# Attention's opening in pieces: halves of K and of the rotation table, Q in two parts, pair 1's Q on GpSimd

## The chip, the cores and the metric

The kernel runs on one core of a Trainium2 chip. The metric is the time of one execution in device microseconds; lower is better. Three executions of the kernel before took 981.68, 982.01 and 981.80 us, median 981.8.

## The reference

The reference is attention with rotary positions, then a mixture of experts that sends each token to one expert, then a dense two-layer block. All is in float32. Cut to what matters here:

```
q_rot, k_rot = rotate(q), rotate(k)          # x1*cos - x2*sin, x1*sin + x2*cos
scores = scale * q_rot @ k_rot.T             # batch 4, 8 heads, 576 tokens, 64 wide
attn = exp(scores - max(scores)); attn /= sum(attn) + 1e-9
x = moe(attn @ v)                            # argmax expert of 8, relu, weighted by its gate
out = relu(x @ w_in)**2 @ w_out              # 2304 tokens, 512 -> 2048 -> 512
```

## The kernel before

The heads are worked off in 16 pairs (P = 0 to 15), two heads on 128 partitions. Q and K of a pair arrive as one block `qk` of 128 x 2 x 2 x 640: the first 2 is the plain copy and the copy with halves swapped, the second is K (index 0) and Q (index 1). `rotate` multiplies both copies with the table `TB` (two `times`) and adds them (one `plus`), in place. The table's Q side is made on ACT from its K side, scaled and moved by 64 columns.

For precision each rotated block is split into a rounded part (`high`, on ACT, into `XH`) and the rest (`low`, into `XL`, on GpSimd unless another engine is named). For pairs 1 and up, `stack_up` lays the parts of one head over each other by ten DMAs on SP's queue (`kZ`, `qZ`, `QH`), so that one matmul does two products. Pair 0 does without: `direct_high` and `direct_low` write its Q parts in place, and its scores take three matmuls instead of two.

Scores come in nine groups s (0 to 3 head 0, 4 to 7 head 1, 8 the last 64 rows of both heads). Each group goes into one of two PSUM buffers `ps` of two banks; VectorE (DVE) takes the row maximum (`smax`, L286), ACT the exponential with its sum (`sexp`, L293), which frees the buffer. Then TensorE (PE) transposes the exponentials (`turn`, L301 and L311), DVE or ACT copies them out (`turned`, L327 and L329), and the product with V follows.

The order on every engine is written out by a list: `at(t, f)` puts a step at a planned time, the list is worked off by time, and each engine runs its instructions strictly in that order. `OFF` has the planned offsets within a pair and the pair's length, 15.954. What `prepare` issues comes ahead of the list. Queues that matter: ACT's order has `high` of pair 2 (planned at 32.143) between pair 1's first maximum (32.353, on DVE) and its first exponential (33.433); GpSimd's (POOL's) order has pair 1's low part and then the three rotation operations of pair 2 (planned from 20.629); SP's has the loads and the stack copies. From pair 2 on, POOL rotates both K and Q of a pair at once, 1280 columns an operation.

In the opening (`prepare`) the table is loaded on ACT's queue and pair 0's K and Q in two transfers on SP's, then pair 1 in one. DVE rotates K, then Q of pair 0, makes the low parts, and rotates pair 1 whole (L433 and L429 are the lines of `times` and `plus`, L425 that of `minus`) ahead of the first row maximum. PE meanwhile runs 14 dummy matmuls (`warm`), and each group of scores of pair 0 has two more ahead of its own (L266).

Of the kernel before, what the change touches and what calls it, by code (L numbers as in the profile page):

```python
# [10 lines left out]
F32 = mybir.dt.float32  # L11
# [48 lines left out]
def shape_constants():  # L60
# [27 lines left out]
    for b in range(B):  # L88
        for c in range(4):
# [21 lines left out]
           un=[32.589, 32.153, 35.217, 38.036, 36.617, 23.748, 28.906, 37.6, 35.653, 34.253, 33.817],  # L111
           out=[33.418, 34.148, 36.917, 39.025, 37.411, 29.788, 32.958, 38.405, 36.294, 35.538, 34.643],
           av=[41.194, 44.969], x=[46.747, 47.789], pj=54.426, fin=58.03)
ON_DVE = [(0, 0), (0, 3), "LQ", "CR", (1, 0), (1, 1), (1, 3)]


def attention(tc, rope, ident, qk, v, w_gate, xd, on_batch, later, ahead):
# [24 lines left out]
    def ppt(name, shape=(128, 512)):  # L142
        return psa.tile(list(shape), F32, name=name, tag="pp", bufs=4)

    def prepare():
        nc.scalar.dma_start(out=TB[:, :, 0], in_=rope)
        load(0)
        load(1)
        for t in Xs:
            nc.gpsimd.memset(t[:, 576:640], 0.0)  # L150
        for t in SS:
            nc.gpsimd.memset(t[:, :, 1:2], 1e-9)
        for two in QH:
            for j in range(2):
                nc.gpsimd.memset(two[j][64 - 64 * j:128 - 64 * j].bitcast(F32), 0.0)
        nc.gpsimd.memset(R, 0.0)
        for r in range(2):
            d = slice(64 * r, 64 * r + 64)
            nc.gpsimd.tensor_copy(R[d, :, r, 0:64], ident[d, d].unsqueeze(1).broadcast_to([64, 4, 64]))
        for o, lo, hi in ((0, 64, 640), (576, 0, 64)):  # L160
            nc.scalar.activation(TB[:, :, 1, o:o + hi - lo], TB[:, :, 0, lo:hi], AF.Copy, scale=0.125)
        for j in range(2):
            Z = T["qZ", j] = zp.tile([128, 640], F32R, name="qZ", tag="qZ", bufs=4)
            nc.gpsimd.memset(Z[64 - 64 * j:128 - 64 * j, 0:512].bitcast(F32), 0.0)
        rotate(0, 0, nc.vector)
        high(0, 0)
        w = ppt("warm")
        for i in range(14):
            nc.tensor.matmul(w, T["hi", 0][:, 0, 0:128], T["hi", 0][:, 0, 0:512], start=True, stop=True)
        rotate(0, 1, nc.vector)  # L170
        direct_high(0)
        low(0, 0, nc.vector)
        direct_low(0, nc.vector)
        load(2)
        rotate(1, None, nc.vector)
        high(1)
        low(1)
        load_v(0)
        stack_up(1)

    def direct_high(P):


        x, h = T["qk", P], T["hi", P]
        for j in range(2):
            r = slice(64 * j, 64 * j + 64)
            nc.scalar.activation(QH[P][j][r], x[r, 0, 1, 0:512], AF.Copy)
        nc.scalar.activation(h[:, 1, 512:640], x[:, 0, 1, 512:640], AF.Copy)

    def direct_low(P, eng):  # L190
        x = T["qk", P]
        for j in range(2):
            r = slice(64 * j, 64 * j + 64)
            minus(eng, T["qZ", 2 * P + j][r, 0:512], x[r, 0, 1, 0:512], QH[P][j][r].bitcast(F32))
        minus(eng, T["lo", P][:, 1, 512:640], x[:, 0, 1, 512:640], T["hi", P][:, 1, 512:640].bitcast(F32))

    def gate_weights():
        for r in range(2):
# [3 lines left out]
    def load(P):  # L202
        t = T["qk", P] = ldp.tile([128, 2, 2, 640], F32, name="qk", tag="qk", bufs=2)
        src = qk[P].rearrange("p (w n c) -> p w n c", w=2, n=2)
        if P == 0:
            for n in range(2):
                nc.sync.dma_start(out=t[:, :, n], in_=src[:, :, n])
        else:
            nc.sync.dma_start(out=t, in_=src)

# [1 line left out]
        V = T["V", P] = wp.tile([128, 2, 5, 64], F32, name="V", tag="V", bufs=2)  # L212
        nc.sync.dma_start(out=V, in_=v[P].rearrange("p (h c d) -> p h c d", h=2, c=5))

    def rotate(P, n, eng, step=None):
        x, a = T["qk", P], slice(0, 2) if n is None else slice(n, n + 1)
        for i, (f, o, y) in enumerate(((times, 0, TB[:, 0, a]), (times, 1, TB[:, 1, a]), (plus, 0, x[:, 1, a]))):
            if step in (None, i):
                f(eng, x[:, o, a], x[:, o, a], y)

    def high(P, n=None):

        if ("hi", P) not in T:
            T["hi", P] = zp.tile([128, 2, 640], F32R, name="XH", tag="XH", bufs=2)
        a = slice(0, 2) if n is None else slice(n, n + 1)
        nc.scalar.activation(T["hi", P][:, a], T["qk", P][:, 0, a], AF.Copy)

    def low(P, n=None, eng=None):
        if ("lo", P) not in T:
            T["lo", P] = zp.tile([128, 2, 640], F32R, name="XL", tag="XL", bufs=2)  # L230
        a = slice(0, 2) if n is None else slice(n, n + 1)
        args = T["lo", P][:, a], T["qk", P][:, 0, a], T["hi", P][:, a].bitcast(F32)
        if eng is None:
            nc.gpsimd.tensor_sub(*args)
        else:
            minus(eng, *args)

    def stack_up(P, n=None):

        h, l = T["hi", P].bitcast(F32), T["lo", P].bitcast(F32)  # L240
        for j in range(2):
            r = slice(64 * j, 64 * j + 64)
            q = nc.scalar if P == 0 and j == 1 else nc.sync
            if n != 1:
                Z = T["kZ", 2 * P + j] = zp.tile([128, 640], F32R, name="kZ", tag="kZ", bufs=4)
                for i in range(2):
                    q.dma_start(out=Z[64 * i:64 * i + 64].bitcast(F32), in_=h[r, 0])
            if n != 0:
                Z = T["qZ", 2 * P + j] = zp.tile([128, 640], F32R, name="qZ", tag="qZ", bufs=4)
                q.dma_start(out=Z[0:64].bitcast(F32), in_=h[r, 1])  # L250
                q.dma_start(out=QH[P % 2][j][r].bitcast(F32), in_=h[r, 1, 0:512])
                q.dma_start(out=Z[64:128].bitcast(F32), in_=l[r, 1])

    def scores(P, s):

        t = T["S", P, s] = ps.tile([128, 2, 512], F32, name="ps", tag="ps", bufs=2)
        if s < 8:
            j, c = divmod(s, 4)
            todo, qs, qh = [j], slice(c * 128, c * 128 + 128), QH[P % 2][j]
            qh = qh[:, qs]  # L260
        else:
            todo, qs, qh = [0, 1], slice(512, 640), T["hi", P][:, 1, 512:640]
        k0 = 0 if s in (4, 5, 6, 7) else 64
        if P == 0:
            for u in range(2):
                nc.tensor.matmul(t[:, u, 0:288], QH[0][0][:, 0:128], T["hi", 0][:, 0, 0:288], start=True, stop=True)  # L266
            H, L = T["hi", P], T["lo", P]
            ql = L[:, 1, 512:640] if s == 8 else T["qZ", 2 * P + j][:, qs]
            for i, (q1, k1) in enumerate(((qh, H), (ql, H), (qh, L))):
                for u in range(2):  # L270
                    nc.tensor.matmul(t[:, u, 0:288], q1, k1[:, 0, k0 + 288 * u:k0 + 288 * u + 288], start=i == 0, stop=i == 2)
            return
        for i, j in enumerate(todo):
            Q1, K1 = T["qZ", 2 * P + j], T["kZ", 2 * P + j]
            for u in range(2):
                nc.tensor.matmul(t[:, u, 0:288], Q1[:, qs], K1[:, k0 + 288 * u:k0 + 288 * u + 288], start=i == 0, stop=False)  # L276
        for u in range(2):
            nc.tensor.matmul(t[:, u, 0:288], qh, T["lo", P][:, 0, k0 + 288 * u:k0 + 288 * u + 288], start=False, stop=True)  # L278
# [103 lines left out]
            at(t, lambda: route(P, t))  # L382

    prepare()
    at(24.0, gate_weights)
    for P in range(NPAIR):
        def on(o, f, *args):
            at(OFF["pair"] * P + o, lambda: f(*args))

        if P > 2:  # L390
            on(OFF["load"], load, P)
        if P > 0:
            on(OFF["v"] + (1.8 if P == NPAIR - 1 else 0), load_v, P)
        if P > 1:
            for i in range(3):
                on(OFF["rope"] + 2.93 * i, rotate, P, None, nc.gpsimd, i)
            on(OFF["hi"], high, P)
            on(OFF["lo"], low, P)
            on(OFF["z"], stack_up, P)
        for s in range(9):  # L400
            on(OFF["S"][s], scores, P, s)
            on(OFF["max"][s], smax, P, s)
            on(OFF["exp"][s], sexp, P, s)
        for un, o, o2 in zip(UNITS, OFF["un"], OFF["out"]):
            on(o, turn, P, un)
# [18 lines left out]
def minus(v, out, a, b):  # L424
    v.tensor_tensor(out=out, in0=a, in1=b, op=ALU.subtract)  # L425
# [839 lines left out]
```

## Time and profile before

| | |
|---|---|
| profiled execution | 982.04 us |
| its span | 980.2 us |
| mean granted clock | 0.997 |
| PE busy | 953.8 us (97%) |
| DVE busy | 531.9 us (54%) |
| ACT busy | 421.5 us (43%) |
| POOL busy | 322.5 us (33%) |

The span is the time from the first to the last instruction of the profiled execution. PE is busy nearly all the time; of the 40 slices of the page only the first has PE at four tenths. The opening is the first 35 us. The four phases after it (the pair loop, routing, experts, dense block) are not touched by the change.

### The profile page before, as it was taken

Reading aid. Unit: us, or ns where it says so; the run is one execution under the profiler, and the core shown is the slowest. Engines: PE = TensorE matmul, PEld = TensorE weight load, DVE = VectorE, ACT = ScalarE, POOL = GpSimd, SP = SyncE. Lnnn points to the kernel's source line nnn. Section 1 sums busy time; section 2 is a strip of 40 time slices with the busy share of each in tenths; the row PEclk is TensorE's granted clock in tenths of the full one; section 3 lists DMA queues with packets and bytes.
Section 4 is the critical chain, followed back from the end, with each engine's and each line's share of the span. In section 5 each row is a group of like instructions: output and inputs, shape, how many; then the busy total and the mean of one; then the engine's idle time right before and its main releaser. Section 6 shows DMA issues by size and latency. Waiting matters only on the chain. (4 is left out here: it accounts for less than half of the span.)

```text
span 980.2 us, 15407 instructions
## 1 busy us (share of the span) xinstructions
PE 953.8 (97%) x5519; PEld 818.1 (83%) x5519; DVE 531.9 (54%) x937; ACT 421.5 (43%) x835; POOL 322.5 (33%) x259
## 2 busy tenths in 40 slices
PE   4999999999999999999999999999999999999997
PEld 4787878788787888888877789999999999999996
DVE  5677877777867255683776479522323323223222
ACT  3676757575642233343464367522222322222221
POOL 4776887887485111251344300010000100100101
PEclk9999999999999999999999999999999999999999
DMA  6876776866542833365377423100100101100000
GB/s 230 238 201 194 231 212 188 256 178 165 183 130 92 303 114 128 107 215 174 130 271 239 160 90 129 33 33 1 38 28 1 65 1 32 34 1 1 33 1 32
DMA packets 45134, 119.80 MB, mean 122 GB/s; under 512 B 8176, under 2 KB 8176, under 8 KB 42608
## 3 DMA queue, kind: packets, MB, share of 16 engines
q1 hardware_dynamic: 39808, 101.58, 33.6%
q0 software_dynamic: 4960, 16.43, 4.9%
q8 instruction: 45, 0.74, 0.3%
q10 hardware_dynamic: 272, 0.66, 0.2%
q14 instruction: 49, 0.40, 0.1%
HBM read 79.93 MB, written 15.11 MB: 97 GB/s over the span
## 5 line engine op out<-in xcount | busy, mean ns | idle before, releaser
L1088 PE MATMUL o<-Wo,gs 128*128 128x512 f32 x864 | 214.5, 393 | 0.0
L1067 PE MATMUL h<-xs,Wi 128*128 128x384 f32 x1008 | 189.6, 336 | 0.0
L1067 PEld LDWEIGHTS h<-xs,Wi 128*128 128x128 f32 x1008 | 178.1, 188 | 6.6
L1088 PEld LDWEIGHTS o<-Wo,gs 128*128 128x128 f32 x864 | 160.0, 188 | 28.3
L1076 DVE SCALAR_TENSOR_TENSOR g<-h,r 128x384 f32<-128x384 f32 x80 | 44.6, 557 | 190.7 <-ACT r L1072 190.7
L293 ACT ACTIVATE e<-ps,mx 128x576 f32<-128x576 f32 x144 | 106.2, 740 | 83.7 <-DVE mx L286 83.5
L1106 POOL DMA_INDIRECT out_dram<-os,at x18 | 17.8, 986 | 369.5 <-DVE os L1101 309.9
L286 DVE TENSOR_REDUCE mx<-ps 128x1 f32<-128x576 f32 x144 | 105.9, 753 | 57.9 <-PE ps L278 50.4
L1072 ACT ACTIVATE r<-h 128x384 f32<-128x384 f32 x96 | 47.1, 490 | 204.7 <-PE h L1067 204.7
L890 PE MATMUL p_y<-W,hh 128*128 128x512 f32 x504 | 123.2, 399 | 1.4 <-ACTq L902 0.8
L861 PE MATMUL p_h<-W,xs 128*128 128x512 f32 x480 | 114.9, 395 | 0.0
L890 PEld LDWEIGHTS p_y<-W,hh 128*128 128x128 f32 x504 | 93.1, 188 | 23.1 <-ACTq L902 1.1
L861 PEld LDWEIGHTS p_h<-W,xs 128*128 128x128 f32 x480 | 88.5, 188 | 18.5 <-DVEq L902 0.7
L311 PE MATMUL pp<-ident,e 128*128 128x128 f32 x640 | 85.4, 273 | 1.3 <-DVE eT L327 1.0
L1078 DVE TENSOR_TENSOR gs<-g,gs 128x384 fp32r<-128x384 f32 x96 | 53.6, 558 | 56.0 <-ACT gs L1077 55.4
L433 POOL TENSOR_TENSOR qk<-qk,TB 128x1280 f32<-128x1280 f32 x28 | 81.4, 2924 | 0.0
L311 PEld LDWEIGHTS pp<-ident,e 128*128 128x128 f32 x640 | 74.4, 141 | 2.6 <-DVE eT L327 1.6
L1077 ACT ACTIVATE gs<-g 128x384 fp32r<-128x384 f32 x96 | 50.4, 525 | 50.4 <-DVE g L1076 49.9
L276 PE MATMUL ps<-kZ,qZ 128*128 128x288 f32 x300 | 71.5, 328 | 0.3
L338 PE MATMUL av<-eT,V 128*64 128x288 f32 x512 | 69.1, 412 | 0.0
L327 DVE COPY eT<-pp 128x512 f32<-128x512 f32 x96 | 64.3, 684 | 4.6 <-PE pp L311 2.7
L895 POOL DMA_INDIRECT yd<-yo,idx x21 | 21.2, 1012 | 124.8 <-DVE yo L894 90.4
(239 smaller groups left out, 1212.2 us busy)
## 6 DMA issues: line engine op xcount, KB each, us to landing
qk<-in_qk_dram SPq DMA_DIRECT2D x15, 1280.0 KB, 7.0
raw<-in_moe_w_dram SPq DMA_DIRECT2D x30, 512.0 KB, 6.5
kZ<-XH SPq DMA_DIRECT2D x60, 160.0 KB, 2.7
rawa<-in_moe_w_dram SPq DMA_DIRECT2D x18, 512.0 KB, 3.9
w<-in_moe_w_in_dram SPq DMA_DIRECT2D x8, 1024.0 KB, 5.2
w<-in_moe_w_out_dram SPq DMA_DIRECT2D x8, 1024.0 KB, 4.9
V<-in_v_dram SPq DMA_DIRECT2D x16, 320.0 KB, 3.0
qZ<-XH SPq DMA_DIRECT2D x30, 160.0 KB, 2.8
```

The costliest lines, as they stand in the source:

```text
L276: nc.tensor.matmul(t[:, u, 0:288], Q1[:, qs], K1[:, k0 + 288 * u:k0 + 288 * u + 288], start=i == 0, stop=False)
L286: nc.vector.tensor_reduce(small("mx", P, 9)[:, s:s + 1], T["S", P, s][:, :, 0:288], axis=AX.XY, op=ALU.max, negate=True)
L293: nc.scalar.activation(ed.rearrange("p (u n) -> p u n", u=2), T["S", P, s][:, :, 0:288], AF.Exp, bias=T["mx", P][:, s:s + 1], accum_out=SS ...
L311: nc.tensor.transpose(t[:, c * 128:c * 128 + 128], src, ident)
L327: nc.vector.tensor_copy(o, i)
L338: nc.tensor.matmul(t[64 * j:64 * j + 64], V[:, j, kc], eT[:, j, kc, cs] if kc < 4 else eL[:, cs], start=kc == 0, stop=kc == 4)
L433: v.tensor_tensor(out=out, in0=a, in1=b, op=ALU.mult)
L861: nc.tensor.matmul(t[u], s[:, a, k], W1[:, b, k, 512 * u:512 * u + 512], start=n == 0, stop=n == 11)
L890: nc.tensor.matmul(t, s[:, a, k], W2[:, b, k], start=n == 0, stop=n == 23)
L1067: nc.tensor.matmul(t, W[:, a, k, fs], s[:, c, k], start=n == 0, stop=n == 11)
L1078: nc.vector.tensor_sub(gs[:, 1], g, gs[:, 0].bitcast(F32))
L1088: nc.tensor.matmul(self.T["o", b][c], gs[:, a, 128 * c:128 * c + 128], W[:, w], start=(f == 0 and n == 0), stop=(f == 15 and n == 2))
```

## The change

- The table is loaded in two halves of 320 columns on ACT's queue; its Q side is made in three pieces instead of two.
- Pair 0's K is loaded in two halves of 320 columns, its Q as part A (256 columns) and part Z (384). Pair 1 is loaded as two transfers, Q first.
- DVE rotates pair 0's K by halves, ACT makes its high part by halves. After the first half come 16 dummy matmuls of 320 columns instead of 14 of 512.
- Q's part A is rotated and split in `prepare`; part Z in the new list `opening`, which has the scores, maxima and exponentials of pair 0 in another order (0, 1, 4, 5, 8, 2, 3, 6, 7) and all of it early in the list.
- The first maxima stand ahead of pair 1's rotation. Pair 1's Q is rotated on POOL (640 columns an operation), its K on DVE in three steps between maxima. High and low parts of pair 1 are made for Q and K apart, the K ones behind the seventh exponential.
- The two dummy matmuls of each group of scores come behind it instead of ahead.
- Four transposes of pair 0 (`FIRST`) move ahead of pair 1's first scores.
- The stack copies of pair 1 issue Q's before K's.

```diff
+FIRST = [(0, 1), (0, 0), (1, 3), (1, 2)]
...
+    HALF, A, Z = (slice(0, 320), slice(320, 640)), slice(0, 256), slice(256, 640)
...
-        nc.scalar.dma_start(out=TB[:, :, 0], in_=rope)
+        for h in HALF:
+            nc.scalar.dma_start(out=TB[:, :, 0, h], in_=rope[:, :, h])
...
-        for o, lo, hi in ((0, 64, 640), (576, 0, 64)):
+        for o, lo, hi in ((0, 64, 320), (256, 320, 640), (576, 0, 64)):
             nc.scalar.activation(TB[:, :, 1, o:o + hi - lo], TB[:, :, 0, lo:hi], AF.Copy, scale=0.125)
...
-        rotate(0, 0, nc.vector)
-        high(0, 0)
-        w = ppt("warm")
-        for i in range(14):
-            nc.tensor.matmul(w, T["hi", 0][:, 0, 0:128], T["hi", 0][:, 0, 0:512], start=True, stop=True)
-        rotate(0, 1, nc.vector)
-        direct_high(0)
+        for h in HALF:
+            rotate(0, 0, nc.vector, cols=h)
+            high(0, 0, h)
+            if h is HALF[0]:
+                T["warm"] = ppt("warm")
+                for i in range(16):
+                    warm(320)
+        rotate(0, 1, nc.vector, cols=A)
+        direct_high(0, A)
         low(0, 0, nc.vector)
-        direct_low(0, nc.vector)
-        load(2)
-        rotate(1, None, nc.vector)
-        high(1)
-        low(1)
-        load_v(0)
-        stack_up(1)
+        direct_low(0, nc.vector, A)
+
+    def warm(n):
+        nc.tensor.matmul(T["warm"][:, 0:n], T["hi", 0][:, 0, 0:128], T["hi", 0][:, 0, 0:n], start=True, stop=True)
+
+    def opening():
...
+        two = lambda s: (lambda: scores(0, s), lambda: smax(0, s), lambda: sexp(0, s))
+        S, M, X = [dict(zip(range(9), [two(s)[n] for s in range(9)])) for n in range(3)]
+        step = lambda i: lambda: rotate(1, 0, nc.vector, i)
+        return [S[0], S[1], lambda: rotate(0, 1, nc.vector, cols=Z), lambda: direct_high(0, Z), M[0], X[0], M[1], X[1],
+                lambda: direct_low(0, nc.vector, Z), lambda: load(2), lambda: rotate(1, 1, nc.gpsimd),
+                S[4], S[5], M[4], X[4], M[5], X[5], step(0), S[8], S[2], M[8], X[8], step(1), lambda: high(1, 1), lambda: low(1, 1),
+                M[2], X[2], step(2), S[3], S[6], M[3], X[3], lambda: high(1, 0), lambda: low(1, 0), lambda: load_v(0), lambda: stack_up(1),
+                M[6], X[6], S[7], M[7], X[7]]
...
-        if P == 0:
-            for n in range(2):
-                nc.sync.dma_start(out=t[:, :, n], in_=src[:, :, n])
+        if P < 2:
+            for n, c in ([(0, h) for h in HALF] + [(1, A), (1, Z)] if P == 0 else [(1, slice(0, 640)), (0, slice(0, 640))]):
+                nc.sync.dma_start(out=t[:, :, n, c], in_=src[:, :, n, c])
...
         if P == 0:
-            for u in range(2):
-                nc.tensor.matmul(t[:, u, 0:288], QH[0][0][:, 0:128], T["hi", 0][:, 0, 0:288], start=True, stop=True)
             H, L = T["hi", P], T["lo", P]
...
+            for u in range(2):
+                warm(288)
             return
...
     prepare()
+    for n, f in enumerate(opening()):
+        at(.1 * n, f)
...
-        for s in range(9):
+        for s in range(9) if P else ():
...
+            if P == 0 and un in FIRST:
+                o, o2 = [t + .2 * FIRST.index(un) for t in (29.5, 29.6)]
```

## Rows read from the trace of the kernel before

**Rows 1.** Busy time by stretch: stretch, length, busy time (instructions) per engine, granted clock, DMA.
```profile
core 0: us, PE busy (x) PEld busy (x) DVE busy (x) ACT busy (x) POOL busy (x), PEclk, DMA share, GB/s
...
50.00:66.00 16.00, 16.00 (x128) 13.04 (x127) 11.81 (x26) 10.52 (x25) 11.17 (x5) 1.00 0.71 194
```

**Rows 2.** Timeline of PE and its weight loads, pair 1's scores s = 8 and 4.
```profile
33.42 0.80 PE L276 MATMUL ps<-kZ,qZ 128*128 128x288 f32 x4
...
35.30 0.30 PEld L276 LDWEIGHTS ps<-kZ,qZ 128*128 128x128 f32 x2 [0.17 <-ACT e L293]
```

**Rows 3.** Timeline of ACT, high part of pair 2.
```profile
33.27 1.26 ACT L226 ACTIVATE XH<-qk 128x1280 fp32r<-128x1280 f32 x1
```

**Rows 4.** Timeline of POOL: pair 1's low part, pair 2's rotation.
```profile
19.90 2.92 POOL L234 TENSOR_TENSOR XL<-qk,XH 128x1280 fp32r<-128x1280 f32 x1 [13.48 <-ACT XH L226]
22.78 5.83 POOL L433 TENSOR_TENSOR qk<-qk,TB 128x1280 f32<-128x1280 f32 x2
28.68 2.94 POOL L429 TENSOR_TENSOR qk<-qk 128x1280 f32<-128x1280 f32 x1
```

**Rows 5.** Timeline of DVE in the opening.
```profile
6.95 1.56 DVE L433 TENSOR_TENSOR qk<-qk,TB 128x640 f32<-128x640 f32 x2 [5.96 <-DMA qk<-in_qk_dram]
...
12.40 1.40 DVE L425 TENSOR_TENSOR qZ<-qk,QH 64x512 fp32r<-64x512 f32 x2
13.83 0.29 DVE L425 TENSOR_TENSOR XL<-qk,XH 128x128 fp32r<-128x128 f32 x1
14.04 2.89 DVE L433 TENSOR_TENSOR qk<-qk,TB 128x1280 f32<-128x1280 f32 x2
...
18.37 1.41 DVE L286 TENSOR_REDUCE mx<-ps 128x1 f32<-128x576 f32 x2
```

**Rows 6.** DMA from 5 to 5.5 us (pair 0) and 8 to 9 (pair 1).
```profile
DMA packets 79, 0.20 MB, mean 404 GB/s; under 512 B 0, under 2 KB 0, under 8 KB 79
...
DMA packets 44, 0.45 MB, mean 451 GB/s; under 512 B 0, under 2 KB 0, under 8 KB 0
```

**Rows 7.** Timelines of DVE and POOL in the experts, where both subtract.
```profile
415.57 1.22 DVE L839 TENSOR_TENSOR W<-rawa,W 128x1024 fp32r<-128x1024 f32 x1 [0.26 <-ACT W L838]
416.57 2.49 POOL L839 TENSOR_TENSOR W<-rawa,W 128x1024 fp32r<-128x1024 f32 x1 [5.92 <-ACT W L838]
417.52 2.63 DVE L839 TENSOR_TENSOR W<-raw,W 128x1024 fp32r<-128x1024 f32 x1 [0.72 <-ACT W L838]
419.02 1.19 POOL L893 COPY yo<-idx 128x16 int32<-128x16 int32 x1
...
499.32 3.60 DVE L839 TENSOR_TENSOR W<-raw,W 128x1024 fp32r<-128x1024 f32 x1
499.42 2.41 POOL L839 TENSOR_TENSOR W<-raw,W 128x1024 fp32r<-128x1024 f32 x1
```

**Rows 8.** Timelines of DVE, ACT and PE, pair 0's scores at full clock.
```profile
28.70 0.76 DVE L286 TENSOR_REDUCE mx<-ps 128x1 f32<-128x576 f32 x1 [0.80 <-PE ps L271]
...
29.49 0.74 ACT L293 ACTIVATE e<-ps,mx 128x576 f32<-128x576 f32 x1 [0.72 <-DVE mx L286]
...
29.18 0.42 PE L271 MATMUL ps<-XH,QH 128*128 128x288 f32 x2
29.45 0.43 PE L271 MATMUL ps<-XH,qZ 128*128 128x288 f32 x2
...
31.75 0.76 DVE L286 TENSOR_REDUCE mx<-ps 128x1 f32<-128x576 f32 x1 [0.81 <-PE ps L271]
```

**Rows 9.** PE's timeline after its gap, and busy time by us around the lower clock.
```profile
20.53 0.53 PE L266 MATMUL ps<-XH,QH 128*128 128x288 f32 x2 [2.56 <-ACT e L293]
...
21.00:22.00 1.00, 1.00 (x9) 1.00 (x8) 0.11 (x1) 0.20 (x2) 1.00 (x1) 0.87 0.88 202
...
25.00:26.00 1.00, 1.00 (x9) 1.00 (x9) 0.35 (x1) 0.41 (x2) 1.00 (x2) 0.92 0.88 233
```

**Rows 10.** Timeline of SP's queue and DMA issues, stack copies of pair 1.
```profile
23.35 1.24 SPq L247 DMA_DIRECT2D kZ<-XH  x2
...
kZ<-XH SPq DMA_DIRECT2D x4, 160.0 KB, 2.4
```

More of the change, by code (lines that the diff above doesn't have):

```diff
@@ L155, in prepare @@
                 nc.gpsimd.memset(two[j][64 - 64 * j:128 - 64 * j].bitcast(F32), 0.0)
+        for j in range(2):
+            q = T["qZ", j] = zp.tile([128, 640], F32R, name="qZ", tag="qZ", bufs=4)
+            nc.gpsimd.memset(q[64 - 64 * j:128 - 64 * j, 0:512].bitcast(F32), 0.0)
         nc.gpsimd.memset(R, 0.0)
@@ L159, in prepare @@
             nc.gpsimd.tensor_copy(R[d, :, r, 0:64], ident[d, d].unsqueeze(1).broadcast_to([64, 4, 64]))
-        for o, lo, hi in ((0, 64, 640), (576, 0, 64)):
+        for o, lo, hi in ((0, 64, 320), (256, 320, 640), (576, 0, 64)):
             nc.scalar.activation(TB[:, :, 1, o:o + hi - lo], TB[:, :, 0, lo:hi], AF.Copy, scale=0.125)
-        for j in range(2):
-            Z = T["qZ", j] = zp.tile([128, 640], F32R, name="qZ", tag="qZ", bufs=4)
-            nc.gpsimd.memset(Z[64 - 64 * j:128 - 64 * j, 0:512].bitcast(F32), 0.0)
@@ L165, in prepare @@
-        rotate(0, 0, nc.vector)
-        high(0, 0)
-        w = ppt("warm")
-        for i in range(14):
-            nc.tensor.matmul(w, T["hi", 0][:, 0, 0:128], T["hi", 0][:, 0, 0:512], start=True, stop=True)
-        rotate(0, 1, nc.vector)
-        direct_high(0)
-        low(0, 0, nc.vector)
-        direct_low(0, nc.vector)
-        load(2)
-        rotate(1, None, nc.vector)
-        high(1)
-        low(1)
-        load_v(0)
-        stack_up(1)
-    def direct_high(P):
+        for h in HALF:
[5 more added lines that the diff above has]
+                    warm(320)
@@ L184, in direct_high @@
+    def direct_high(P, cols):
         x, h = T["qk", P], T["hi", P]
+        to = min(cols.stop, 512)
         for j in range(2):
             r = slice(64 * j, 64 * j + 64)
-            nc.scalar.activation(QH[P][j][r], x[r, 0, 1, 0:512], AF.Copy)
-        nc.scalar.activation(h[:, 1, 512:640], x[:, 0, 1, 512:640], AF.Copy)
-    def direct_low(P, eng):
+            nc.scalar.activation(QH[P][j][r, cols.start:to], x[r, 0, 1, cols.start:to], AF.Copy)
+        if cols.stop > 512:
+            nc.scalar.activation(h[:, 1, 512:640], x[:, 0, 1, 512:640], AF.Copy)
@@ L191, in direct_low @@
+    def direct_low(P, eng, cols):
         x = T["qk", P]
+        to = min(cols.stop, 512)
         for j in range(2):
             r = slice(64 * j, 64 * j + 64)
-            minus(eng, T["qZ", 2 * P + j][r, 0:512], x[r, 0, 1, 0:512], QH[P][j][r].bitcast(F32))
-        minus(eng, T["lo", P][:, 1, 512:640], x[:, 0, 1, 512:640], T["hi", P][:, 1, 512:640].bitcast(F32))
+            minus(eng, T["qZ", 2 * P + j][r, cols.start:to], x[r, 0, 1, cols.start:to], QH[P][j][r, cols.start:to].bitcast(F32))
+        if cols.stop > 512:
+            minus(eng, T["lo", P][:, 1, 512:640], x[:, 0, 1, 512:640], T["hi", P][:, 1, 512:640].bitcast(F32))
@@ L213, in load_v, with rotate, high @@
         nc.sync.dma_start(out=V, in_=v[P].rearrange("p (h c d) -> p h c d", h=2, c=5))
-    def rotate(P, n, eng, step=None):
+    def rotate(P, n, eng, step=None, cols=slice(0, 640)):
         x, a = T["qk", P], slice(0, 2) if n is None else slice(n, n + 1)
-        for i, (f, o, y) in enumerate(((times, 0, TB[:, 0, a]), (times, 1, TB[:, 1, a]), (plus, 0, x[:, 1, a]))):
+        for i, (f, o, y) in enumerate(((times, 0, TB[:, 0, a, cols]), (times, 1, TB[:, 1, a, cols]), (plus, 0, x[:, 1, a, cols]))):
             if step in (None, i):
-                f(eng, x[:, o, a], x[:, o, a], y)
-    def high(P, n=None):
+                f(eng, x[:, o, a, cols], x[:, o, a, cols], y)
+    def high(P, n=None, cols=slice(0, 640)):
         if ("hi", P) not in T:
@@ L225, in high @@
         a = slice(0, 2) if n is None else slice(n, n + 1)
-        nc.scalar.activation(T["hi", P][:, a], T["qk", P][:, 0, a], AF.Copy)
+        nc.scalar.activation(T["hi", P][:, a, cols], T["qk", P][:, 0, a, cols], AF.Copy)
     def low(P, n=None, eng=None):
@@ L236, in low, with stack_up @@
             minus(eng, *args)
-    def stack_up(P, n=None):
+    def stack_up(P):
         h, l = T["hi", P].bitcast(F32), T["lo", P].bitcast(F32)
@@ L242, in stack_up @@
             r = slice(64 * j, 64 * j + 64)
[L243 to L252, printed above, removed]
+            k = T["kZ", 2 * P + j] = zp.tile([128, 640], F32R, name="kZ", tag="kZ", bufs=4)
+            q = T["qZ", 2 * P + j] = zp.tile([128, 640], F32R, name="qZ", tag="qZ", bufs=4)
+            todo = [(q[0:64], h[r, 1]), (QH[P % 2][j][r], h[r, 1, 0:512]), (q[64:128], l[r, 1])]
+            ks = [(k[64 * i:64 * i + 64], h[r, 0]) for i in range(2)]
+            for o, i in todo + ks if P == 1 else ks + todo:
+                nc.sync.dma_start(out=o.bitcast(F32), in_=i)
     def scores(P, s):
```

## The prediction

> **What bounds the kernel now.** I read the page, then the busy table by stretches, then each engine's timeline up to 36 us. The table shows TensorE (PE) busy 16.00 of 16 us in a stretch of the pair loop [rows 1], so once the loop runs, what arrives late stays late and what arrives early stays early. The change touches only the opening, so the question is when that full stretch begins. PE's timeline shows it: pair 1's scores for s = 8 start at 33.42, and those for s = 4 start at 35.30 after a short wait for ACT [rows 2]. I take the start of pair 1's s = 4 as the gauge, **G = 35.30**. In both versions the same work lies before it on PE: pair 0's nine scores, its LQ, CR and the four transposes of FIRST, and pair 1's s = 2 and s = 8. After it the order is the same. So the change is worth the shift of G, and a transpose done earlier gains nothing if G does not move.
>
> G hangs on ACT: the s = 4 scores need the PSUM buffer that the exp of pair 1's s = 2 reads, and in ACT's order that exp stands right behind high(2), which ran from 33.27 to 34.53 [rows 3]. high(2) needs pair 2's rotated Q and K: three GpSimd (POOL) operations of some 2.9 us each that ended at 31.62, queued behind pair 1's low part, which ran from 19.90 [rows 4]. Thus POOL was 1.65 us ahead of ACT. Whoever comes last at high(2), ACT or POOL, sets G, 0.77 us after the end of high(2).
>
> **The change part by part.**
>
> *Loads by halves.* K's two halves carry the bytes of before; K's reader started at 6.95 then [rows 5]. Runs of 2560 bytes (79 packets, 0.20 MB) moved 404 GB/s, runs of 10240 bytes 451 [rows 6]. A straight line through the time per run gives about 357 for runs of 1280 bytes, which puts K's second half near 7.4; with no loss it is 6.95. I take 7.0, by the row. The Trainium skill (DMA: Bandwidth & Descriptors, Specifications) states that line rate is reached from 512 bytes up. The two rows differ by a tenth far above that size, so the trace doesn't quite agree. By the rule K is there at 6.95, by the line at 7.4, and the sum moves by under half a us.
>
> *DVE up to the first maximum.* 640 columns took 0.78 us (two in 1.56), 512 took 0.715 from start to start, 128 took 0.21 [rows 5]; that makes about 0.42 for 320, 0.36 for 256 and 0.50 for 384. From 7.0: K's second half, three operations of 320, 1.3 (8.3); Q's part A, three of 256, 1.1 (9.4); low of K 0.8 (10.2); the two low parts of A 0.7 (10.9); Q's part Z, three of 384, 1.5 (12.4). In the new order the first maximum stands behind all of these, so DVE alone would reach it at 12.4, against 18.37 before [rows 5]. The warm matmuls start when ACT has K's first half and end near 11.7 by my estimate (16 of 320 columns at the lower clock), so they don't hold it.
>
> *Pair 1's Q on GpSimd.* Three operations, each half of 2.92 us: 4.4 us on an engine that was idle there. But DVE does not run beside it. A DVE subtraction with two SBUF inputs, 1.22 us at 415.57, took 2.63 when it started at 417.52 inside a POOL subtraction that ran until 419.06; then DVE ran, and POOL's next copy (16 columns) took until 420.21. One that started at 499.32 took 3.60 because a POOL subtraction started at 499.42 [rows 7]. So two such operations exclude each other and take turns. Q of pair 1 is the fourth transfer; two of 0.66 MB after K's, at 0.41 MB/us, put it near 10. DVE then still has the low of K, two low parts and three rotation steps, all with two SBUF inputs, and all three POOL operations fall between them: first maximum at 12.4 + 4.4 = 16.8. Bounds 12.4 (nothing lost) and 16.8; a gain is excluded, since DVE loses no work before its first maximum by it. I take 16.8, by the three cases.
>
> *From there to the exp of s = 3.* K's high of pair 1 stands on ACT behind the seventh exp. Two PSUM buffers alternate; before, every second maximum came 3.05 us after the first (28.70 to 31.75), with the two dummy matmuls ahead of each score taking 0.27 [rows 8]. They move behind, so a round is 2.78. The exp starts 0.79 after its maximum and takes 0.74 [rows 8]. The seventh is in the fourth round: 3 x 2.78 + 0.79 + 0.74 = 9.9. DVE's steps on pair 1's K (0.8 each) and ACT's high of its Q (0.74) stick out of a round by some 0.45: 10.3. ACT's high of Q's part Z, 1.1 us behind the rotation, delays the first exp by 0.35. And PE stands idle between the second scores and the first exp, from about 14 to 19: before, after 2.56 idle us that ended at 20.53, the granted clock fell to 0.50 (1.2 GHz) at about 21.74 and rose at about 25.16 [rows 9]. That is 3.4 us at half speed, of which I charge a quarter, 0.8, since PE is not all the bound here. 16.8 + 10.3 + 0.35 + 0.8 = 28.3.
>
> *POOL then.* K's high on ACT 0.85 with its wait, K's low on POOL half of 2.92 and the handing over: 30.7. Only now does pair 2's rotation start, since it stands behind both low parts in POOL's queue: 30.7 + 8.84 = 39.55 (before 22.78 + 8.84 = 31.62 [rows 4]). ACT is at high(2) some 7 us earlier and waits; behind it wait the exp, the PSUM buffer and PE. high(2) ends at 39.55 + 0.05 + 1.26 = 40.85, against 34.53: **6.3 us late**.
>
> *PE's clock again.* The stack copies of pair 1 now have K's high (29.2) in front of seven of the ten: 0.62 us each to issue, 2.4 to land [rows 10], the last near 36. s = 8 runs then, and PE waits to 41.6, longer than the gap that brought half clock before. 3.4 us of it in a stretch that PE bounds cost half: **1.7 us** (bounds 0, if the clock holds, and 2.3).
>
> Sum 6.3 + 1.7 = 8.0. The profiled execution took 982.04 (span 980.2), 0.24 above the median of 981.8, so I forecast 981.8 + 8.0 = **989.8 us**.
>
> What I cost at nothing: the table's extra activation (some 0.3 us) lies in ACT's wait for DMA; if it did not, the warm matmuls would start that much later, and they have 0.3 us to spare. load(2) and V issue on SP ahead of the stack copies, whose data come later; without that cover they cost two issues, 1.2 us.
>
> **Rivals.**
>
> *DVE goes first.* If DVE's queued operations keep POOL out, the first maximum is at 12.4 and POOL's three run beside the maxima, which read PSUM. K's low then ends at 12.4 + 0.35 + 10.3 + 2.4 = 25.5, the rotation at 34.3, high(2) at 35.6: 1.1 late, and PE still waits about 5 us ahead of s = 4, 1.7 more: 984.6 (982.9 without the clock). For it: no row has a long chain on DVE against POOL. Against it: at 499.32 DVE was there first and still waited [rows 7]. The Trainium skill (SBUF — State Buffer, Who interferes with whom) says that issue order decides who blocks; by that DVE, always queued, would go first here and the time would be this rival's. The row at 499.32 speaks against it.
>
> *No change.* POOL is blocked in part and PE keeps its clock, so that high(2) comes within 1.9 us of before: 981 to 983.7.
>
> *Faster.* The stall at high(2) does not arise. Its place is the end of K's low on POOL, its point 24.4 (34.53 - 1.31 - 8.84). Every us below that is gained, until the stack copies hold s = 8: they would land near 31, 33.42 - 31 = 2.4, so at best 979.4. For it the first maximum must come by 11.3 and nothing collide; DVE's chain alone ends at 12.4, so K's second half would have to be there at 5.9, ahead of its bytes at the rate of before, or the maxima closer than the round above.
>
> *Halves don't come sooner.* If both halves land together, warm matmuls and first scores start a us later and DVE's end at 12.4 stays, since it hangs on the second half: inside the range.
>
> **How the numbers follow.** Forecast (they take turns, 987 to 992): 0.62. DVE first or mostly so (983.8 to 987): 0.20. No change (979.9 to 983.7): 0.11. Faster: 0.07. A measurement of this kernel can tell about 0.2% from no change, 1.96 us; so slower 0.82, same 0.11, faster 0.07. The range 983 to 992 leaves out faster, most of no change and a tail above: under 2 in 10.
>
> **What would show it.** In the profile after: DVE operations of 1.8 us and more beside three POOL operations between 10 and 17; the first maximum near 17; pair 2's first rotation on POOL at 30 or later; high(2) on ACT behind an idle stretch that POOL ends; PE idle for several us ahead of pair 1's s = 4, then half clock. The forecast is wrong if K's low on POOL ends before 26 or s = 4 starts before 37. If DVE's operations keep their lengths, the 4.4 us are wrong; if PE's gaps close the delay after 42, so is the claim that the loop keeps what the opening loses.

## The result: 989.5 us, 0.8% slower, by way of GpSimd's queue

| | before | after |
|---|---|---|
| median (lowest to highest of 4) | 981.90 us (981.68 to 982.54) | 989.45 us (988.00 to 990.12) |
| profiled execution, its span | 982.04, 980.2 | 988.00, 986.2 |
| mean granted clock | 0.997 | 0.993 |

The ratio is 1.0076, 95% interval [1.0064, 1.0088]: slower, 0.35 us below the forecast of 989.8.

DVE and POOL after, in the opening (timelines: start, duration, engine, line, operation, idle time and its releaser):

```profile
7.42 0.90 DVE L452 TENSOR_TENSOR qk<-qk,TB 128x320 f32<-128x320 f32 x2 [0.40 <-DMA TB<-in_rope_dram]
...
10.62 2.10 DVE L444 TENSOR_TENSOR qZ<-qk,QH 64x256 fp32r<-64x256 f32 x2
12.76 3.64 DVE L452 TENSOR_TENSOR qk<-qk,TB 128x384 f32<-128x384 f32 x2
16.43 0.56 DVE L448 TENSOR_TENSOR qk<-qk 128x384 f32<-128x384 f32 x1
16.90 1.41 DVE L301 TENSOR_REDUCE mx<-ps 128x1 f32<-128x576 f32 x2
...
25.92 1.98 POOL L253 TENSOR_TENSOR XL<-qk,XH 128x640 fp32r<-128x640 f32 x1 [9.94 <-ACT XH L245]
28.71 1.55 POOL L253 TENSOR_TENSOR XL<-qk,XH 128x640 fp32r<-128x640 f32 x1 [0.82 <-DMA QH<-XH]
30.22 5.76 POOL L452 TENSOR_TENSOR qk<-qk,TB 128x1280 f32<-128x1280 f32 x2
36.06 2.89 POOL L448 TENSOR_TENSOR qk<-qk 128x1280 f32<-128x1280 f32 x1
```

The first maximum comes at 16.90, 1.47 earlier than in [rows 5]. POOL's low part of pair 1, one operation that ended at 22.8 in [rows 4], is now two, and the second ends at 30.26. Pair 2's rotation stands behind it and ends at 38.95 instead of 31.62. On ACT and PE:

```profile
27.91 0.73 ACT L245 ACTIVATE XH<-qk 128x640 fp32r<-128x640 f32 x1
...
38.98 1.27 ACT L245 ACTIVATE XH<-qk 128x1280 fp32r<-128x1280 f32 x1 [6.36 <-POOL qk L448]
...
36.73 0.50 PE L291 MATMUL ps<-kZ,qZ 128*128 128x288 f32 x2 [2.78 <-DMA kZ<-XH]
37.06 0.42 PE L293 MATMUL ps<-XL,XH 128*128 128x288 f32 x2
41.02 0.85 PE L291 MATMUL ps<-kZ,qZ 128*128 128x288 f32 x2 [3.54 <-ACT e L308]
...
48.17 2.16 PE L353 MATMUL av<-eT,V 128*64 128x288 f32 x16
```

high(2) waits 6.36 us for POOL, where [rows 3] has no idle time ahead of it, and s = 4 of pair 1, 35.30 in [rows 2], starts at 41.02. Ahead of it PE stood idle twice, 2.78 us for a stack copy and 3.54 us for ACT's exp. The busy time by us (columns PE, PEld, DVE, ACT, POOL, granted clock, DMA share, GB/s) shows the clock at the lower of its two levels, 1.2 GHz (0.50, from 38 to 44, so also in the first three us of the new work), and a full stretch of 16 us later, as in [rows 1]:

```profile
37.00:38.00 1.00, 0.48 (x4) 0.25 (x2) 0.48 (x1) 0.00 (x0) 1.00 (x1) 0.75 1.06 440
...
43.00:44.00 1.00, 1.00 (x6) 1.00 (x6) 0.14 (x1) 0.82 (x3) 1.00 (x2) 0.50 0.96 219
44.00:45.00 1.00, 1.00 (x10) 1.00 (x8) 0.90 (x2) 0.50 (x2) 1.00 (x1) 0.84 0.92 199
...
60.00:76.00 16.00, 16.00 (x128) 13.05 (x127) 11.81 (x26) 10.52 (x26) 11.18 (x5) 1.00 0.70 197
```

Whether the loop keeps the delay is read from one row: all products with V (`av`) by line, with the start of the first and of the last. Before, and after:

```profile
L338 PE MATMUL av<-eT,V x512: 405/406/458, 41.0 to 294.1; 128*64 128x288 f32 x171
```

```profile
L353 PE MATMUL av<-eT,V x512: 406/406/457, 48.2 to 301.2; 128*64 128x288 f32 x171
```

The first (48.17 against 41.05) and the last are 7.1 us late. From the last to the first product of the dense block (567.7 before, 573.6 after) 1.2 us come back; they make the difference between 7.1 and the 5.96 us of the two profiled executions.

### The profile page after: what moved, and what is told of

Read it like the earlier page. It is cut to its first block, busy times and chain, and to the rows that moved or that the text cites. A ratio compares the mean times of both kernels' runs of the same rounds, so it can differ in the third digit from the quotient of the medians.

```text
span 986.2 us, 15440 instructions
## 1 busy us (share of the span) xinstructions
PE 954.6 (97%) x5521; PEld 819.9 (83%) x5521; DVE 534.3 (54%) x945; ACT 422.3 (43%) x840; POOL 329.1 (33%) x263
## 5 line engine op out<-in xcount | busy, mean ns | idle before, releaser
L1107 PEld LDWEIGHTS o<-Wo,gs 128*128 128x128 f32 x864 | 160.0, 188 | 28.3
L452 POOL TENSOR_TENSOR qk<-qk,TB 128x1280 f32<-128x1280 f32 (+1 forms) x30 | 84.7, 2843 | 4.1 <-DMA qk<-in_qk_dram 4.1
L291 PEld LDWEIGHTS ps<-kZ,qZ 128*128 128x128 f32 x300 | 45.5, 191 | 22.6 <-issue 9.8
```

The source lines that it names most:

```text
L452: v.tensor_tensor(out=out, in0=a, in1=b, op=ALU.mult)
L1107: nc.tensor.matmul(self.T["o", b][c], gs[:, a, 128 * c:128 * c + 128], W[:, w], start=(f == 0 and n == 0), stop=(f == 15 and n == 2))
```

## The experiments

All kernels in one table. s = 4 is the start of pair 1's scores s = 4; "first and last product" are the two starts of the row above. Both are from the one profiled execution, which need not be the median one (halves_only's, 982.29 us, was the fastest of its seven, q_on_dve's, 988.88, the slowest of its five). Times are medians beside runs of the kernel before on the same chip (981.49 to 981.90 us).

| kernel | s = 4 | first, last product | time (executions) | ratio to before, 95% |
|---|---|---|---|---|
| before | 35.30 | 41.0, 294.1 | 981.5 | |
| after | 41.02 | 48.2, 301.2 | 989.45 (4) | 1.0064 to 1.0088 |
| after_timed (after again) | 41.27 | 49.6, 303.1 | 990.11 (5) | 1.0067 to 1.0094 |
| low_on_dve | 46.19 | 52.3, 305.4 | 991.60 (4) | 1.0085 to 1.0119 |
| q_on_dve | 39.59 | 47.9, 301.0 | 987.08 (5) | 1.0042 to 1.0070 |
| k_first | 38.34 | 46.6, 300.0 | 986.87 (5) | 1.0045 to 1.0071 |
| warm_gap | 42.14 | 47.9, 301.0 | 990.44 (6) | 1.0070 to 1.0101 |
| warm_gap_timed | 41.52 | 47.3, 300.4 | 989.89 (5) | 1.0072 to 1.0100 |
| k_first_warm | 38.82 | 44.5, 297.6 | 985.95 (5) | 1.0042 to 1.0070 |
| halves_only | 36.37 | 42.1, 295.3 | 983.83 (7) | 1.0016 to 1.0041 |
| pool_short | 37.63 | 44.0, 298.3 | not usable, see there | |
| before_behind | 34.40 | 40.1, 293.3 | 980.63 (11) | 0.9983 to 1.0001 |
| before_fill | 33.74 | 39.5, 292.7 | 980.29 (12) | 0.9979 to 0.9996 |

In every row but pool_short's the last product is as late or early as the first, to within 0.4 us: what the opening loses, the pair loop keeps.

**Do DVE and POOL take turns?** Three kernels tell. q_on_dve takes POOL out of the opening:

```diff
-                ... lambda: load(2), lambda: rotate(1, 1, nc.gpsimd),
-                S[4], S[5], M[4], X[4], M[5], X[5], step(0), ...
+                ... lambda: load(2), qstep(0),          # qstep(i): one operation of rotate(1, 1, nc.vector)
+                S[4], S[5], M[4], X[4], qstep(1), M[5], X[5], qstep(2), step(0), ...
```

> Pair 1's Q is rotated on VectorE in three steps between maxima, no longer on GpSimd; the low parts stay on GpSimd. Theory P with the collision: the first maximum comes near 12.7 instead of 16.9, K's low part ends near 27 instead of 30.26 (three more VectorE steps between the maxima cost about 1 us), high(2) ends near 37, s = 4 starts near 38: 986 us. Rival (GpSimd and VectorE don't exclude each other in the opening; the first maximum is late for another reason, such as data that come late): the first maximum stays near 16.9 and the time near 989.

987.08 us, where 986 was expected and the rival had 989; s = 4 came at 39.59 instead of 38. DVE's timeline:

```profile
10.76 0.86 DVE L445 TENSOR_TENSOR qZ<-qk,QH 64x256 fp32r<-64x256 f32 x2
11.66 1.03 DVE L453 TENSOR_TENSOR qk<-qk,TB 128x384 f32<-128x384 f32 x2
12.72 0.56 DVE L449 TENSOR_TENSOR qk<-qk 128x384 f32<-128x384 f32 x1
15.02 0.76 DVE L302 TENSOR_REDUCE mx<-ps 128x1 f32<-128x576 f32 x1 [1.74 <-PE ps L285]
```

The same operations take 0.86 and 1.03 us instead of 2.10 and 3.64. The 3.85 us between the two pairs are what POOL's rotation took from DVE. The first maximum, expected at 12.7, then waits for PE until 15.02 (PE's first scores ran at the lower clock here, 0.68 us for 0.43), so of the 3.85 only 1.88 show in it.

k_first keeps POOL's rotation but lets its data come later:

```diff
-    ... else [(1, slice(0, 640)), (0, slice(0, 640))]   # pair 1: Q, then K
+    ... else [(0, slice(0, 640)), (1, slice(0, 640))]   # pair 1: K, then Q
```

> The kernel after, with pair 1's K loaded ahead of its Q. Q then lands one transfer (0.66 MB at 0.41 MB/us, 1.6 us) later, so GpSimd's first operation on it would start near 12.35 instead of 10.75. By the theory (operations with two SBUF inputs of VectorE and GpSimd take turns) VectorE has done its two low parts by 11.5 and most of part Z by then, loses at most one turn of 1.7 us, and the first maximum waits for TensorE near 15.0 as with Q on VectorE; K's low on GpSimd ends near 28.6, s = 4 of pair 1 starts near 39.3: 987 us (986.5 to 987.5). By the rival, that GpSimd's rotation costs VectorE its whole 4.4 us wherever it lies, or that some other part of the opening holds the maxima, the first maximum stays near 17 and the time at 989.4.

986.87 us, as expected. DVE, POOL and ACT:

```profile
10.60 0.86 DVE L444 TENSOR_TENSOR qZ<-qk,QH 64x256 fp32r<-64x256 f32 x2
11.49 1.03 DVE L452 TENSOR_TENSOR qk<-qk,TB 128x384 f32<-128x384 f32 x2
12.55 1.95 DVE L448 TENSOR_TENSOR qk<-qk 128x384 f32<-128x384 f32 x1
14.42 1.41 DVE L301 TENSOR_REDUCE mx<-ps 128x1 f32<-128x576 f32 x2
15.76 2.13 DVE L444 TENSOR_TENSOR qZ<-qk,QH 64x256 fp32r<-64x256 f32 x2
...
12.54 3.37 POOL L452 TENSOR_TENSOR qk<-qk,TB 128x640 f32<-128x640 f32 x2 [5.57 <-DMA qk<-in_qk_dram]
...
36.30 1.27 ACT L245 ACTIVATE XH<-qk 128x1280 fp32r<-128x1280 f32 x1 [6.37 <-POOL qk L448]
```

POOL starts at 12.54 instead of 10.75, and ahead of the first maximum only the DVE operation that begins beside it is stretched, 1.95 instead of 0.56. Behind the first two maxima the low part of Z meets POOL's last operation (15.99 to 17.61) and takes 2.13 instead of 0.86. So 1.39 us are lost before the first maximum and 2.66 in all, instead of 3.85. The rival, that the rotation costs the first maximum its whole length wherever it lies, falls. PE's idle stretch of 3.32 us ahead of the third scores became two of 1.30 and 0.93, and the granted clock read 1.00 in each us from 18 to 25, where after had 0.50 from 21 to 23; so K's low part ends 2.7 us earlier than in after (27.59), though the first maximum is only 2.5 us earlier.

low_on_dve was to shorten POOL's queue:

```diff
-    lambda: low(1, 1), ... lambda: low(1, 0),
+    lambda: low(1, 1, nc.vector), ... lambda: low(1, 0, nc.vector),
```

> The two low parts of pair 1 go from GpSimd to VectorE; all else as in the changed kernel. Theory P (the loss is GpSimd's queue: pair 2's rotation stands behind K's low part): pair 2's rotation starts as soon as its data are there, near 25 instead of 30.2, high(2) ends near 35.5 instead of 40.25, and the s = 4 scores of pair 1 start near 37.5, now held by the stack copies that s = 8 waits for (36.7 in the changed kernel): 985 to 986 us. Rival S (the stack copies, or the new order of scores, are the limit by themselves): s = 4 stays near 41 and the time near 989.

991.60 us: a miss, the slowest usable time of all. POOL's queue was free as meant, and pair 2's rotation started at 25.25. But it ran into what DVE still had to do:

```profile
25.35 3.52 DVE L452 TENSOR_TENSOR qk<-qk,TB 128x640 f32<-128x640 f32 x1
28.79 3.49 DVE L444 TENSOR_TENSOR XL<-qk,XH 128x640 fp32r<-128x640 f32 x1
32.20 0.74 DVE L301 TENSOR_REDUCE mx<-ps 128x1 f32<-128x576 f32 x1
32.87 2.84 DVE L448 TENSOR_TENSOR qk<-qk 128x640 f32<-128x640 f32 x1
...
25.25 6.36 POOL L452 TENSOR_TENSOR qk<-qk,TB 128x1280 f32<-128x1280 f32 x2 [9.26 <-DMA qk<-in_qk_dram]
31.68 3.35 POOL L448 TENSOR_TENSOR qk<-qk 128x1280 f32<-128x1280 f32 x1
```

Each DVE operation of 0.8 us waits out one POOL operation of 2.9. The maximum at 32.20, which reads PSUM alone, keeps its 0.74. POOL ends at 35.03, but the exps are now late and ACT reaches high(2) only at 43.67; the stack copies, which stand behind K's high part (37.15), are later still, PE waits for them until 45.59, and s = 4 starts at 46.19. My expectation had freed one queue without asking what its next work would collide with.

**Is it POOL's queue that sets s = 4?** pool_short drops two thirds of pair 2's rotation:

```diff
-                on(OFF["rope"] + 2.93 * i, rotate, P, None, nc.gpsimd, i)
+                if P > 2 or i == 2:
+                    on(OFF["rope"] + 2.93 * i, rotate, P, None, nc.gpsimd, i)
```

> The kernel after, but of the three GpSimd operations of pair 2's rotation the two multiplications are left out (the output of pair 2 is then wrong). By the prediction's step (GpSimd's queue holds high(2), and that alone sets s = 4) high(2) comes 5.8 us earlier, s = 4 starts near 35.3, and the time is 982 to 982.5. By the trace of after there is a second wait right behind it: the second half of s = 8 on TensorE stood at 36.73, waiting for the stack copies (kZ), so s = 4 can't start before some 37.5, and with the half clock that follows such an idle stretch (1.4 to 1.7 us) the time is 985 to 986. If GpSimd's queue is not what sets it, 989.

Its time, 1027.5 us, can't be used: with pair 2's values wrong the experts' stage has other work. Its second-layer products p_y run from 327.2 to 612.0 (in after from 319.9 to 572.1), and ACT rounds blocks of expert weights 72 times instead of 32. The opening's trace can be used. ACT and PE:

```profile
33.31 1.27 ACT L245 ACTIVATE XH<-qk 128x1280 fp32r<-128x1280 f32 x1 [0.55 <-POOL qk L449]
...
36.53 0.82 PE L291 MATMUL ps<-kZ,qZ 128*128 128x288 f32 x2 [2.71 <-DMA kZ<-XH]
37.15 0.68 PE L293 MATMUL ps<-XL,XH 128*128 128x288 f32 x2
37.63 0.68 PE L291 MATMUL ps<-kZ,qZ 128*128 128x288 f32 x2
```

high(2) runs at 33.31, where it ran before [rows 3], yet s = 4 starts at 37.63, not at 35.30. Of the 5.72 us of delay POOL's queue alone holds the last 3.39; behind it lies a second wait that costs 2.33 by itself, the stack copies of pair 1's K (half a us of it is the lower clock: 1.10 us from the end of the wait to s = 4, where low_on_dve, at full clock, took 0.60). This is the expectation's second case, which had 37.5. In after SP issues the last of them until 33.91, since they stand behind K's high part on ACT (27.91), they land 3.3 us after their issue (median; 2.4 in [rows 10]), and PE waits until 36.73.

**What does the granted clock cost?** warm_gap fills PE's two idle stretches ahead of s = 4 with dummy matmuls:

```diff
+    def gap_warm(n):
+        if n == 20:
+            T["warm"] = ppt("warm")
+        for i in range(n):
+            warm(288)
...
+    at(32.9, lambda: gap_warm(20))          # behind s = 2
+    at(34.0, lambda: gap_warm(24))          # behind s = 8
```

> Dummy matmuls of 288 columns fill TensorE's two idle stretches ahead of pair 1's s = 4 (20 between s = 2 and s = 8, 24 behind s = 8). Theory: high(2) and the start of s = 4 stay at 40.3 and 41.0, but the clock is not granted at half from 41 to 44, so the loop runs 1.4 us earlier: about 988.0 us. Rival (the half clock costs nothing, since ACT is as full there): 989.4.

The clock stayed at 1.00 from 30 to 45, and s = 4 to the first product took 5.76 us (42.14 to 47.90), as before (35.30 to 41.05); after had taken 7.15. But the time was 990.44, no better than after. In the profiled execution 1.12 us of that went ahead of the dummies: the clock read 0.50 from 18 to 24 (in after from 21 to 23), K's low part ended at 31.27 instead of 30.26, and s = 4 started that much later. So the same edit was timed beside after itself, and once more on k_first (9 and 30 dummies, `n == 9`):

> The kernel after, unchanged, timed beside the next two on one chip, as their measure: 989.4 us (988 to 990), first av product at 48.2.

> The dummy matmuls of warm_gap once more, now beside after itself. In the trace of warm_gap the clock stayed at 1.00 and the stretch from s = 4 of pair 1 to the first av product took 5.76 us instead of 7.15; its time was no shorter, but its profiled execution lost 1.8 us between the last av product and the first of the next stage (p_y). Theory: the 1.4 us are real and that loss is scatter, so it is 988.0, 1.4 under after. Rival: the dummies themselves cost as much (they hold s = 8 or s = 4 back, or what follows): 989.4 or more.

> k_first (986.87, first av product at 46.62) with 9 dummy matmuls of 288 columns between pair 1's s = 2 and s = 8 and 30 behind s = 8, in TensorE's idle stretches of 1.42 and 4.37 us. Theory: the granted clock, 0.50 until 44.3 there, stays at 1.00; the score and transpose work from 38.3 to 44.3 ran at half speed, 2.5 us too long by the same work's 5.76 us from s = 4 to the first av product, so the first av product comes near 44.1 and the time near 984.4. Rival: it doesn't show in the time: 986.9.

The first of these is PE in after_timed, the second in warm_gap_timed, the third in k_first_warm, at s = 4:

```profile
41.27 0.85 PE L291 MATMUL ps<-kZ,qZ 128*128 128x288 f32 x2 [4.42 <-ACT e L308]
```

```profile
41.52 0.53 PE L297 MATMUL ps<-kZ,qZ 128*128 128x288 f32 x2
```

```profile
38.82 0.42 PE L297 MATMUL ps<-kZ,qZ 128*128 128x288 f32 x2
```

Their first products stand at 49.6, 47.3 and 44.5: 8.3, 5.8 and 5.6 us behind. So the clock cost 1.4 us in one execution of after and 2.5 in another (there it read 0.50 until 47), and the dummies take all of it away: the last products are 2.7 us (300.4 against 303.1) and 2.4 us (297.6 against 300.0) earlier than without them. The times are not. 989.89 against 990.11, and 985.95 against 986.87 in another series, are inside the scatter. Both theories missed; warm_gap_timed is its rival's 989.4 or more, k_first_warm lies between the two. Most of the gain goes between the last product with V and the first product of the dense block: 272.4 and 272.8 us in after's two profiles and 272.6 in k_first, but 275.9, 275.1 and 274.0 in the three with dummies. The other kernels take 272.4 to 273.8 there (before 273.6, q_on_dve 273.6), so only warm_gap's two lie clearly outside. One piece of it is seen in all three, in the routing stage. In k_first, then in k_first_warm:

```profile
315.35 1.03 POOL L452 TENSOR_TENSOR xs<-xs,gate 128x480 fp32r<-128x480 f32 x1 [1.04 <-DVE xs L458]
315.53 1.37 DVE L452 TENSOR_TENSOR xs<-xs,gate 128x480 fp32r<-128x480 f32 x1
```

```profile
313.54 0.66 DVE L460 TENSOR_TENSOR xs<-xs,gate 128x480 fp32r<-128x480 f32 x1
313.66 1.43 POOL L460 TENSOR_TENSOR xs<-xs,gate 128x480 fp32r<-128x480 f32 x1 [1.33 <-DVE xs L466]
...
315.14 2.42 PE L714 MATMUL p_r<-xs,row 128*128 128x72 f32 x20 [0.40 <-POOL xs L460]
```

With the dummies DVE comes first, POOL's half waits, and PE waits 0.40 for it; from the experts' first product p_y to the first p_y of their second layer it is 9.3 us in all three instead of 8.6 to 8.7 in every other kernel but pool_short. Why, stays open, and so does where the rest goes (1.6 us in warm_gap_timed, 0.7 in k_first_warm). One candidate that no run separates from the dummies: `gap_warm` also takes a new PSUM tile out of the four that the later work uses in turn, so every later tile lands in another one. before_fill (below) has its dummies in an old tile, and 8.7 there.

**What do the other parts do alone?** halves_only keeps the pieces (loads, table, pair 0 by halves and parts, 16 dummies) and goes on as before: pair 1 whole, one transfer, rotated on DVE ahead of the maxima.

```diff
         direct_low(0, nc.vector, A)
+        rotate(0, 1, nc.vector, cols=Z); direct_high(0, Z); direct_low(0, nc.vector, Z)
+        load(2); rotate(1, None, nc.vector); high(1); low(1); load_v(0); stack_up(1)
...      # pair 1's load, its stack copies, the dummies of each score and the transposes as before
-    for n, f in enumerate(opening()): at(.1 * n, f)
...
```

> Only the pieces: table and K by halves, Q of pair 0 in two parts, all of it ahead of the scores, and 16 shorter dummy matmuls; pair 1's rotation whole on VectorE, order of scores, low parts, dummy matmuls per score and transposes as before. Theory: VectorE is through with pair 0 1.4 us earlier (12.7 instead of 14.04), pair 1's rotation, its low part on GpSimd and pair 2's rotation follow 1.4 us earlier, and s = 4 of pair 1 starts near 33.9: 980.5 us. Rival (smaller transfers cost what the pieces gain, or the scores are held by the dummy matmuls): 981.8.

983.83 us: slower than before, a miss; s = 4 is 1.07 us late instead of 1.4 early. Its DVE and PE:

```profile
12.58 0.56 DVE L453 TENSOR_TENSOR qk<-qk 128x384 f32<-128x384 f32 x1
13.62 0.87 DVE L449 TENSOR_TENSOR qZ<-qk,QH 64x256 fp32r<-64x256 f32 x2 [0.48 <-ACT QH L212]
...
19.06 1.41 DVE L310 TENSOR_REDUCE mx<-ps 128x1 f32<-128x576 f32 x2
...
21.22 0.85 PE L290 MATMUL ps<-XH,QH 128*128 128x288 f32 x2 [5.21 <-ACT e L317]
```

The first maximum is 0.69 later than in [rows 5]: the pieces add operations, each with its fixed share (two of 256 and 384 columns take 0.42 and 0.56, one of 640 took 0.82), and DVE waits 0.48 for ACT between them. Meanwhile PE's first scores come earlier, so it idles 5.21 us instead of 2.56 [rows 9] and its first two matmuls after that take 0.85 us instead of 0.53. Earlier scores without an earlier maximum only lengthen PE's wait.

before_behind and before_fill work on the kernel before. The first moves the two dummies of each score behind it:

```diff
-            for u in range(2):
-                nc.tensor.matmul(t[:, u, 0:288], QH[0][0][:, 0:128], T["hi", 0][:, 0, 0:288], start=True, stop=True)
+            warm(2)          # after the score's matmuls, into the tile of the first dummies
...
+    at(17.1, lambda: warm(18))          # before_fill alone
```

> The kernel before, with one part of the change alone: the two dummy matmuls of each of pair 0's scores stand behind the score instead of ahead of it. By the prediction's step a round of two scores takes 2.78 us instead of 3.05; three rounds give 0.8 us, ScalarE reaches high(2) at 32.5 instead of 33.27, GpSimd (done at 31.62) doesn't hold it: 981.0 us. Rival: the round is set by the exp and the maximum, the dummies cost nothing: 981.8.

> As before_behind, and 18 dummy matmuls of 288 columns (2.4 us) in TensorE's idle stretch from 17.98 to 20.53, so that the granted clock does not fall to 0.50 from 21.7 to 25.2. That takes 1.2 to 1.4 us of waiting out of ScalarE's second to fourth exp; ScalarE would reach high(2) near 31.3, GpSimd holds it to 31.65, s = 4 of pair 1 starts near 33.8 instead of 35.30: 980.3 us, the fastest of these kernels. Rival: the clock falls all the same, or something later takes the gain back: 981 to 981.8.

980.63 and 980.29 us. The first is not clear of the kernel before (0.9983 to 1.0001), though high(2) starts at 32.37, where its theory has 32.5; the second is faster than the kernel before, by 0.13% [0.04%, 0.21%], as expected. Between the two the times don't decide. high(2) on ACT, in before_behind, then in before_fill:

```profile
32.37 1.26 ACT L230 ACTIVATE XH<-qk 128x1280 fp32r<-128x1280 f32 x1
```

```profile
31.70 1.27 ACT L230 ACTIVATE XH<-qk 128x1280 fp32r<-128x1280 f32 x1
```

The first is 0.90 earlier than in [rows 3], and s = 4 as well (34.40). In the second the granted clock reads 1.00 from 17 to 29, where before had half clock [rows 9], and high(2) starts at 31.70, right as POOL ends (31.67): ACT has caught up with POOL, and s = 4 has gained 1.56 of the 1.65 us by which POOL was ahead.

## Why the prediction was right

| step | predicted | measured |
|---|---|---|
| K's second half on DVE | 7.0 | 7.42, behind the table's second half |
| DVE to the end of part Z, undisturbed | 12.4 | 13.14 (halves_only) |
| taken by POOL's three operations | 4.4 | 3.85 |
| first maximum | 16.8 | 16.90 |
| a round of two scores | 2.78 [rows 8] | 2.80 (exps at 24.38 and 27.18) |
| exp of s = 3 ends | 28.3 | 27.92 |
| K's low on POOL ends | 30.7 | 30.26 |
| pair 2's rotation ends | 39.55 | 38.95 |
| s = 4 of pair 1, later by | 6.3 | 5.72 (after_timed 5.97) |
| half clock from there | 1.7 | 1.40 (after_timed 2.5) |
| sum, first product | 8.0 | 7.12 (after_timed 8.6) |
| profiled execution | 8.0 | 5.96 (after_timed 8.07) |
| time, median | 8.0 | 7.55 |

The path of the delay is shown: turns by q_on_dve and k_first, POOL's queue by the opening of pool_short, the lower clock by the filled gaps, the loop's memory by the table of products. Not shown is that the clock's share reaches the time: filling the gaps won 2.7 and 2.4 us at the last product, and 0.2 and 0.9 us, inside the scatter, in the medians. The Trainium skill (SBUF — State Buffer, Who interferes with whom) says that an instruction with two SBUF inputs on VectorE and one of GpSimd that reads SBUF contend, and that one holds the other off for a whole instruction; the stretched rows (0.56 to 1.95, 0.8 to 3.5) and the untouched maxima (0.74) agree.

The turns are the smaller part of the loss. With them gone or fewer, s = 4 comes 1.43 us (q_on_dve) and 2.68 us (k_first) earlier, of 5.72, and high(2) still waits 6.4 us for POOL in both: the larger part is the new order, which puts K's high and low part behind the seventh exp and pair 2's rotation behind that.

Three terms were mis-sized. DVE's chain was 0.7 too short: 0.42 is K's second half (at 7.42 behind the table's second half; at 7.45 in halves_only, there behind DVE's own work on the first half), the rest are small operations a little longer than my straight line through three sizes. The turns were 0.55 too dear, and by luck the two errors cancelled in the 16.8. And I charged the whole delay to POOL. I had put the last stack copy near 36 and then used that only for the clock; pool_short shows that it holds s = 4 at 37.63 with POOL out of the way. It did not change the time, since the two waits lie beside each other, but a repair of POOL's queue alone would have been forecast 2.3 us too good.

"DVE goes first" fell on the 2.10 and 3.64. That halves don't come sooner was half true: K's first half let DVE start at 5.32, but pieces cost more than they brought. Q of pair 1 is the fifth transfer, not the fourth; its place near 10 came from the bytes and held (POOL began on it at 10.75). The prediction said nothing of the path behind the loop, which took 272.4 to 275.9 us from kernel to kernel (pool_short aside), a spread above several terms of the sum. That the median came within 0.35 us of the forecast is therefore in part luck: in one profile of after the clock cost 1.4 and that path gave 1.2 us back, in the other the clock cost 2.5.

## What to carry to other kernels

Before work is moved to GpSimd, list what VectorE does in the same microseconds with two SBUF operands, and what already stands in GpSimd's queue: here one move paid both. A start that comes earlier is worth nothing until the last of the waits ahead of the full stretch moves, so look for the second-latest wait as well. Idle gaps on TensorE have a second price in the clock after them, 1.4 to 2.5 us of work here. Filling them is not sure to pay: 18 dummy matmuls in one gap and 18 moved behind their scores brought the kernel before to 980.3, the fastest here, while in the changed kernel the filled gaps did not show in the time.

## What was not expected of the hardware

- The same kernel in two executions: after stood idle 2.78 and 3.54 us ahead of s = 4 in one profile, 1.42 and 4.42 us in the other. The granted clock was back within the us from 44 and within the us from 47, 1.4 and 2.5 us of work lost. q_on_dve and k_first, with last gaps of 4.11 and 4.37 us, also took 8.3 us from s = 4 to the first product.
- Which of two colliding engines goes first follows the records only loosely. In the routing stage the one with the earlier start, by 0.12 and 0.18 us, went undisturbed, as the Trainium skill has it (SBUF — State Buffer, Who interferes with whom: the order of issue decides); in [rows 7] DVE started 0.10 ahead and still waited.
- Dummy matmuls at 35 us, with a PSUM tile of their own, went with a routing stage 280 us later that took 0.6 to 0.7 us longer in all three kernels that had them. before_fill, with its dummies at 17 us in an old tile, had 8.7 us there as before. What does it is not shown.
